# Attention and gated feed-forward in one kernel: which tokens go through plain matrix products, which through Strassen units, and how many DMAs turn a pair of heads

## The chip, the cores and the metric

One core of one Trainium2 chip runs the whole program. The metric is the device time of one execution in microseconds (us), as the median of several runs. One execution of each kernel is also recorded by the hardware profiler. Engines are named as in the profile: PE is TensorE (matrix products), ACT is ScalarE, DVE is VectorE, POOL is GpSimd, SP is the engine that only issues DMAs.

## The reference

```python
batch, n_heads, seq, head_dim = (8, 12, 448, 64)
n_tokens, d_model, d_ff = (3584, 768, 1536)

def _attn_ref(q, k, v):
    scores = 1.0 / np.sqrt(q.shape[-1]) * np.matmul(q, k.transpose(0, 1, 3, 2))
    scores = scores - np.max(scores, axis=-1, keepdims=True)
    attn = np.exp(scores)
    attn = attn / (np.sum(attn, axis=-1, keepdims=True) + 1e-09)
    return np.matmul(attn, v)

def _moe_ref(x, w_gate, w_val, w_out):     # x: the heads side by side, 3584 x 768
    g = x @ w_gate
    silu = g * (1.0 / (1.0 + np.exp(-g)))
    return (silu * (x @ w_val)) @ w_out    # 3584 x 768, float32
```

## The kernel before

Everything is computed in float16 with float32 accumulation. The order of all engines' work is written out by hand; nothing is reordered later except where a small planner sorts a list of items.

**Attention.** The 96 heads form 48 pairs, six to a batch. A pair's q, k and v are loaded and cast on GpSimd's DMA queue (`load_qk16` L186, `load_v` L205), from pair 16 on into a ring of four places (`rawslot` L182, `RL` L23) and nine places for v (`VS` L31). From pair 11 on GpSimd copies q and k into one tile (`prep_quad` L233; two copies) and SP turns them by DMA transposes, one for k and one for q (L239, L243), into `qkT`, five buffers. For each chunk of keys PE makes scores into a PSUM tile `s` of two banks (`qk_quad` L324; three such tiles rotate), and ACT takes the exponential into a ring `E` (L349). Then PE multiplies by v (`pv_mm` L413, 32 matmuls of 65 columns per pair), DVE divides by the sums (`pv_close` L444), and the result `xt` is turned into `X`, from pair 12 on by two DMA transposes on SP: 384 tokens (L494) and the last 64 (L498). `X` has two buffers, each for two batches (896 tokens, "kk").

**Feed-forward, plain.** `Step` (L546) makes one of the 12 row blocks of the gate and value products for up to 512 tokens: six matmuls each, a tanh on ACT, two products on DVE, result in `hts`. `block` (L873) gives the steps of a token block: the even blocks are 384 tokens, the odd ones 512, so blocks 0 and 1 are batches 0 and 1, blocks 2 and 3 are batches 2 and 3, and so on.

**Feed-forward, Strassen.** `Unit` (L763) makes two row blocks of one product for 2 x w tokens with seven half-size products instead of eight; 12 units (six for the gate, six for the value) cover all rows. They need sums of weights (`weight_sums` L753, on POOL), sums of token columns (`token_sums` L988, on DVE) and additions on DVE. `unit_items` (L1319) lists their pieces with engines and durations and `order_of` (L43) sorts them. The output product uses the same scheme: `out_group` (L672) makes 256 tokens x 384 columns in 42 matmuls of 192 columns; it is a generator with two halves (18 and 24 matmuls). Sums for it come from `h_sums` (L535) and `out_sums` (L523). Rows that don't fill a group go through `plain_out` (L642, 192 or 384 columns) or `single_out` (L1002).

**The stages.** From 26 us on the pairs go through a `plan` (L1163) of visits: three chunks of scores, then usually one pair's products with v, then items of feed-forward work. Every seventh visit is bare, without a pair's products. From visit 19 on `VISITS` (L978) says for each visit how many plain steps and how many whole groups run (`run_pair` L1027 makes two steps with the second one split in halves, `run_group` L1069 and `run_group_with` L1090 put a group around a step or a pair's products). Blocks 0 to 4 are plain. After the last exponential come: units of width 256 for block 5 (the last 64 tokens of batch 4 and batch 5), three pairs of groups, units of width 448 for batches 6 and 7 with one `single_out` row block between them, and three pairs of groups for these.

Of the kernel before, what the change touches and what calls it, by code (L numbers as in the profile page):

```python
# [30 lines left out]
VS = 9  # L31
# [33 lines left out]
def kernel(  # L65
# [44 lines left out]
    xp = ctx.enter_context(tc.tile_pool(name="xp", bufs=2))  # L110
    fp = ctx.enter_context(tc.tile_pool(name="fp", bufs=2))
    ps_s = ctx.enter_context(tc.tile_pool(name="ps_s", bufs=3, space=PSUM))
    ps_f = ctx.enter_context(tc.tile_pool(name="ps_f", bufs=2, space=PSUM))
# [10 lines left out]
    warm = consts.tile([128, 128], FP16, name="warm")  # L124
    warm4 = warm[:].unsqueeze(1).to_broadcast([128, 4, 128])
# [22 lines left out]
    hall = consts.tile([128, NFB * NB * S], FP16, name="hts")  # L148

# [4 lines left out]
    wo = [wo_all[:, i] for i in range(2)]  # L154

    raw = {}
    qkT = {}
    X = {}

    def dummy(n, w=4):  # L160
        wp = ps_f.tile([128, 512], FP32, tag="f", name="wp")
        for _ in range(n):
            nc.tensor.matmul(wp[:, 0 : w * 128], lhsT=warm[:], rhs=warm4[:, 0:w], start=True, stop=True)
# [17 lines left out]

    def rawslot(pr):  # L182
        a, b = divmod(pr % RS if pr < 2 * RS else pr % RL, 2)
        return raws_all[:, a, :, b]

    def load_qk16(pr, n=2):  # L186
        for t, src in ((0, q), (1, k)):
            if pr >= QUAD and t:
                if n == 1:
                    kd = rawslot(pr)[:, 1].rearrange("p (h x) -> p h x", h=2)  # L190
                else:
                    kd = raws_all[:, pr % RS // 2, 1].rearrange("p b (h x) -> p (b h) x", h=2)
                load_keys(nc.gpsimd, kd, k, 2 * pr, 2 * n)
                continue
# [3 lines left out]
            else:  # L198
                dst = raws_all[0:P, pr % RS // 2, t].rearrange("p b (h x) -> p (b h) x", h=2)
# [5 lines left out]
    def load_v(pr, n=1):  # L205
        b, h = divmod(2 * pr, H)
# [26 lines left out]
    def prep_quad(pr):  # L233
        rq, rk = raw[pr]
        qk16 = attp.tile([128, 2, NC, 2, D], FP16, tag="qk16", name="qk16", bufs=3)
# [12 lines left out]
    def prep(pr):  # L248
# [3 lines left out]
        if pr == 0 or pr >= NPE:  # L252
            qk16 = attp.tile([128, 2, NC, 2, D], FP16, tag="qk16", name="qk16", bufs=3)[0:P]
# [7 lines left out]
        qkT[pr] = attp.tile([128, 2 * S + D], FP16, tag="qkT", name="qkT", bufs=QB)  # L261
# [11 lines left out]
        def turn0():  # L273
            for t in range(2):
                tp = ps_s.tile([128, 2, 512], FP32, tag="s", name="tp")
# [17 lines left out]
        def turn():  # L293
            if pr < WIDE + 2:
                tp = ps_s.tile([128, 2, 1024], FP16, tag="s", name="tp")[:, 0]
            else:
                tp = ps_f.tile([128, 1024], FP16, tag="f", name="tp")
# [25 lines left out]

    def qk_quad(pr, c):  # L324
        s = ps_s.tile([128, 2, 512], FP32, tag="s", name="s")
        if c < KR:
            t = qkT[pr]
            for hx in range(2):
                nc.tensor.matmul(  # L329
                    s[:, hx, 0:S],  # L330
                    lhsT=t[ts(hx, 64), ts(c + low(pr, hx), 128)],
                    rhs=t[ts(hx, 64), ds(NC * 128, S)],
# [3 lines left out]
        else:  # L336
            for hx in range(2):
                for p in (pr, pr + 1):
# [3 lines left out]
                        s[ts(1 - lo, 64), hx, 0:S],  # L342
                        lhsT=t[ts(hx, 64), ds(0 if lo else KR * 128 + 64, 64)],
                        rhs=t[ts(hx, 64), ds(NC * 128, S)],
# [8 lines left out]
    def qk(pr, c):  # L353
# [3 lines left out]
        s = ps_s.tile([128, 2, 512], FP32, tag="s")  # L357
# [19 lines left out]
    def pv_chunk(pr, c):  # L377
        if c == 0:
            accs[pr] = ps_f.tile([128, 512], FP32, tag="f", name="acc")
# [48 lines left out]
    def pv_open(pr, one=False):  # L428
        if one:
            acc = ps_s.tile([128, 2, 512], FP32, tag="s", name="acc")  # L430
            accs[pr] = [acc[:, hx] for hx in range(2)]
        else:
            accs[pr] = [ps_f.tile([128, 512], FP32, tag="f", name="acc") for _ in range(2)]
# [1025 lines left out]
```

## Time and profile before

| what | value |
|---|---|
| median of three runs (lowest, highest) | 429.64 us (429.29, 430.12) |
| span of the profiled execution | 428.2 us |
| matmuls | 4635 |
| last exponential ends | 300 us |
| TensorE busy from 83.6 to 300.1 us | 215.7 of 216.5 us |
| TensorE busy from 300.1 us to the end | 124.0 of 128.1 us |
| DMA, mean over the span | 117 GB/s |

The span is that of one profiled execution; the runs' times hold a little more than the span. "Busy" is the union of an engine's instructions; matmuls overlap in a pipeline, so what a matmul costs is the distance from one start to the next, and not its listed mean duration. A turn is a DMA transpose: SP spends about 1.25 us to issue it, and it lands some time later; the landing is what a waiting engine sees.

### The profile page before, as it was taken

To read this page: it belongs to the slowest core of one execution; us is meant where nothing else is said; L and a number is where in the kernel's file an instruction comes from. 1 tells how busy PE (TensorE), PEld (TensorE's weight loads), DVE (VectorE), ACT (ScalarE), POOL (GpSimd) and SP (SyncE) were. 2 spreads that over 40 slices of the span, in tenths; PEclk is the share of its full clock that TensorE was granted. 3 is DMA by queue.
4 is the path that set the end of the run, shared out by engine and by line. 5 is a ranking of instruction groups with operands and counts; after the bars stand their busy time and mean duration, and the time that the engine had idled before them with its cause. 6 is when DMAs were issued, how large, how long until landed. Compare 5 with 4: busy or idle time off the path is not lost.

```text
span 428.2 us, 11621 instructions
## 1 busy us (share of the span) xinstructions
PE 420.5 (98%) x4635; PEld 290.2 (68%) x4635; DVE 267.7 (63%) x642; ACT 245.2 (57%) x395; POOL 233.3 (54%) x358
## 2 busy tenths in 40 slices
PE   8999999999999999999999999999999999999996
PEld 3666656555557777747666677777888995555795
DVE  4666562576758665575545776567777765565663
ACT  6975667556566645546667556568655225545221
POOL 8756543999887583658543885934999000000001
PEclk9999999999999999999999999999999999999999
DMA  9999999999999999999999999823100331000125
GB/s 138 177 200 200 199 173 190 121 169 209 160 138 137 115 146 150 146 136 120 124 151 122 139 149 117 152 45 97 25 1 14 101 99 51 0 0 2 38 76 148
DMA packets 108551, 50.02 MB, mean 117 GB/s; under 512 B 60864, under 2 KB 105232, under 8 KB 108496
## 3 DMA queue, kind: packets, MB, share of 16 engines
q0 software_dynamic: 46944, 24.83, 54.0%
q1 hardware_dynamic: 61408, 24.27, 33.6%
q8 instruction: 36, 0.59, 0.7%
q14 instruction: 19, 0.16, 0.1%
q10 hardware_dynamic: 144, 0.17, 0.1%
HBM read 49.55 MB, written 11.01 MB: 141 GB/s over the span
## 4 chain that ended last, share of the span: by engine, by line
PE 77%; DMA 15%; POOL 4%; DVE 1%; ACT 1%; issue 1%; SPq 0%; POOLq 0%; DVEq 0%
PE og L679 18%; PE gp L557 15%; PE un L795 10%; PE vp L557 9%; PE acc L420 8%; PE ub L795 8%; PE s L329 5%; DMA wv<-in_moe_w_val_dram 4%; DMA qkraw<-in_q_dram 4%; DMA qkraw<-in_k_dram 3%; DMA wg<-in_moe_w_gate_dram 2%; PE op L650 2%; POOL qkraw L200 2%; DMA qkT<-qk 1%; PE s L341 1%; PE op L1003 1%
## 5 line engine op out<-in xcount | busy, mean ns | idle before, releaser
L349 ACT ACTIVATE E<-s 128x896 f16<-128x896 f32 x126 | 106.6, 918 | 40.2 <-PE s L329 28.2
L557 PE MATMUL gp<-X,wg 128*128 128x384 f16 (+1 forms) x360 | 73.9, 347 | 0.0
L237 POOL COPY qk<-qkraw 128x512 f16<-128x512 f16 x72 | 43.7, 649 | 50.8 <-DMA qkT<-qk 48.9
L557 PE MATMUL vp<-X,wv 128*128 128x384 f16 (+3 forms) x360 | 66.7, 321 | 0.1
L610 DVE SCALAR_TENSOR_TENSOR t<-sg,gp 128x384 f32<-128x384 f32 (+1 forms) x60 | 36.3, 607 | 42.5 <-ACT sg L584 42.2
L557 PEld LDWEIGHTS <-wv 128*128 128x128 f16 x462 | 43.8, 98 | 25.8 <-issue 0.3
L640 POOL DMA_DIRECT2D out_dram<-osb x3 | 1.6, 541 | 90.9 <-ACT osb L698 90.9
L177 POOL DMA_DIRECT2D vraw<-in_v_dram x72 | 43.8, 629 | 12.8 <-DVE X L492 6.9
L557 PEld LDWEIGHTS <-wg 128*128 128x128 f16 x360 | 32.8, 98 | 26.1 <-issue 1.9
L584 ACT ACTIVATE sg<-gp 128x384 f32<-128x384 f32 (+1 forms) x60 | 32.1, 537 | 28.8 <-PE gp L557 28.1
L177 POOL DMA_DIRECT2D qkraw<-in_k_dram x70 | 42.4, 619 | 7.7 <-DMA wo<-in_moe_w_out_dram 4.7
L367 ACT ACTIVATE E<-s 112x896 f16<-112x896 f32 x48 | 40.5, 919 | 8.5 <-PE s L359 8.3
L420 PEld LDWEIGHTS <-E 128*128 128x128 f16 (+1 forms) x1152 | 37.4, 96 | 10.9 <-issue 4.7
L679 PEld LDWEIGHTS <-hts 128*128 128x128 f16 x528 | 44.1, 98 | 0.3
L420 PE MATMUL acc<-vo,E 128*128 128x65 f16 (+1 forms) x1152 | 42.3, 192 | 0.7 <-DVE X L492 0.3
L616 DVE SCALAR_TENSOR_TENSOR hts<-t,vp 128x384 f16<-128x384 f32 (+3 forms) x60 | 32.5, 541 | 5.5 <-PE vp L557 1.9
L698 ACT ACTIVATE osb<-og 128x384 f32<-128x384 f32 x22 | 10.8, 491 | 39.4 <-PE og L679 37.5
L200 POOL DMA_DIRECT2D qkraw<-in_q_dram x44 | 29.9, 680 | 5.4 <-DMA vraw<-in_v_dram 1.4
L450 DVE TENSOR_TENSOR xt<-acc,R 128x256 f16<-128x256 f32 x72 | 30.6, 425 | 2.5
L329 PE MATMUL s<-qkT 64*128 64x448 f16 x216 | 30.4, 354 | 0.6 <-DMA qkT<-qk 0.5
L679 PE MATMUL og<-wo,hts 128*128 128x192 f16 x264 | 29.0, 246 | 0.0
L679 PEld LDWEIGHTS <-hsum 128*128 128x128 f16 x300 | 25.5, 98 | 1.0
(180 smaller groups left out, 723.8 us busy)
## 6 DMA issues: line engine op xcount, KB each, us to landing
vraw<-in_v_dram POOLq DMA_DIRECT2D x72, 64.0 KB, 4.9
qkraw<-in_q_dram POOLq DMA_DIRECT2D x41, 112.0 KB, 4.8
qkraw<-in_k_dram POOLq DMA_DIRECT2D x68, 64.0 KB, 4.8
wg<-in_moe_w_gate_dram POOLq DMA_DIRECT2D x8, 288.0 KB, 9.7
wv<-in_moe_w_val_dram POOLq DMA_DIRECT2D x8, 288.0 KB, 10.2
wo<-in_moe_w_out_dram POOLq DMA_DIRECT2D x2, 1152.0 KB, 19.4
out_dram<-osb SPq DMA_DIRECT2D x7, 288.0 KB, 4.1
out_dram<-osb SPq DMA_DIRECT2D x6, 336.0 KB, 3.2
```

The costliest lines, as they stand in the source:

```text
L177: eng.dma_start(dst[ts(s, 64)], rows)
L200: nc.gpsimd.dma_start(dst, flat.rearrange("h (p c) d -> p h (c d)", c=NC))
L237: nc.gpsimd.tensor_copy(dst.rearrange("p c h d -> p h c d"), src)
L329: nc.tensor.matmul(s[:, hx, 0:S], lhsT=t[ts(hx, 64), ts(c + low(pr, hx), 128)], rhs=t[ts(hx, 64), ds(NC * 128, S)], start=True, stop=True,)
L349: nc.scalar.activation(e[:, 0 : 2 * S].rearrange("p (h q) -> p h q", h=2), s[:, :, 0:S], AF.Exp, scale=sm_scale)
L367: nc.scalar.activation(e[:, :, 0:S], s[0:P, :, 0:S], AF.Exp, scale=sm_scale)
L420: nc.tensor.matmul(acc[:, ts(j, D + 1)], lhsT=e[rows, ds(hx * S + j * 128, 128)], rhs=Vts[pr % NV][rows, hx, col, 0 : D + 1], start=first, ...
L557: nc.tensor.matmul(dst[:, 0:w], lhsT=wslice(kind, self.fb, cb), rhs=X[kk][:, cb, ds(c0 + lo, w)], start=(cb == 0), stop=(cb == NCB - 1),)
L610: nc.vector.scalar_tensor_tensor(self.t1[:, 0:n], self.sg[:, 0:n], 1.0, self.gp[:, 0:n], ALU.add, ALU.mult)
L616: nc.vector.scalar_tensor_tensor(self.hts[:, self.fb, ds(lo, w)], self.t1[:, ds(lo, w)], 0.5 * HS, vp[:, 0:w], ALU.mult, ALU.mult)
L679: nc.tensor.matmul(dst, lhsT=lhs(n), rhs=rhs(n), start=first and n == 0, stop=n == NH - 1, skip_group_check=True)
L795: mm = nc.tensor.matmul(dst, lhsT=lhs[:, n], rhs=rhs[:, n], start=first and n == 0, stop=n == NK - 1, skip_group_check=True,)
```

## The change

The diff does five things.

1. Only blocks 0, 1 and 2 (batches 0 and 1, and 384 tokens of batch 2) are plain. After the last exponential come three unit stages: batches 4 and 5 (width 448), then the last 64 tokens of batch 2 with batch 3 (width 256), then batches 6 and 7 (width 448). Each is followed by its groups. The 512 tokens of batches 2 and 3 leave `X` before pair 36 overwrites it: SP writes them to DRAM in visit 26 (`spill`) and reads them back behind the first unit stage. Two of the three token sums move from DVE to POOL.
2. A visit has one item: a step (`S`), the first or the second half of a group (`1`, `2`), or a quarter-row output product (`Q`).
3. A pair's q and k are turned by one DMA. A pair's `xt` is turned by one DMA of four blocks, which writes 64 columns more than the pair has; the pair after it overwrites them. Batch 3 (odd, in the first pair of buffers) keeps two DMAs.
4. From pair 16 on, q, k and v are loaded for two pairs at a time.
5. PSUM tiles come from a hand-written rotation, so that a group that is held over two visits keeps its tile while the others go round. The copies `p1` and `p15` of a group live in its output tile.

```diff
-VS = 9
+VS = 10
...
+    dram = ctx.enter_context(tc.tile_pool(name="dram", bufs=1, space=bass.MemoryType.DRAM))
...
+    order_in = {"s": [0, 1, 2], "f": [0, 1]}
+    lent = {}
+    def bank(kind, name, shape, dtype, hold):
+        slots = order_in[kind]
+        at = slots.pop(0)
+        t = ps.tile(list(shape), dtype, tag=f"{kind}{at}", name=name)
+        if hold:
+            lent[id(t)] = (slots, at, t)
+        else:
+            slots.append(at)
+        return t
...
     def load_v(pr, n=1):
+        if pr % VS + n > VS:
+            fit = VS - pr % VS
+            load_v(pr, fit)
+            return load_v(pr + fit, n - fit)
...
     def prep_quad(pr):
...
-        qkT[pr] = attp.tile([128, NC * 128 + S], FP16, tag="qkT", name="qkT", bufs=QB)
+        qkT[pr] = attp.tile([128, 2 * NC * 128], FP16, tag="qkT", name="qkT", bufs=QB)
         nc.sync.dma_start_transpose(
-            qkT[pr][:, 0 : NC * 128].rearrange("p (c q) -> p c q", q=128),
-            qk16[:, 0].rearrange("p c h d -> p (c h d)"),
-        )
-        nc.sync.dma_start_transpose(
-            qkT[pr][:, NC * 128 :].rearrange("p (c q) -> p c q", q=P),
-            qk16[0:P, 1].rearrange("p c h d -> p (c h d)"),
+            qkT[pr][:].rearrange("p (c q) -> p c q", q=128),
+            qk16[:].rearrange("p t c h d -> p (t c h d)"),
         )
...
     def turn_x(pr):
...
+        if kk > 1 or not bb:
+            at = (bb * NCB + hp) * S if kk > 1 else hp * NB * S
+            nc.sync.dma_start_transpose(
+                Xflat[kk][:, ds(at, (KR + 1) * 128)].rearrange("p (j q) -> p j q", q=128),
+                xt[:].rearrange("p j d -> p (j d)"),
+            )
+            return
...
     def out_group(kk, c0, hts, t, at, qw, osb, last=False, own=False, mid=None):
...
-        g = ps_s.tile([128, 2, 512], FP32, tag="s", name="og")
+        g = two_banks("og", hold=True)
...
-        p1 = fp.tile([128, QW], FP32, tag="p1", name="p1")
-        p15 = fp.tile([128, QW], FP32, tag="p15", name="p15")
+        p1 = osb[1][:, ds(qw * OH, QW)]
+        p15 = osb[1][:, ds(qw * OH + QW, QW)]
...
         def add_block(i, visits):
-            if i < B - NB - 1:
+            if i < NB + 1:
...
-        FIRST_STEPS = [2, 2, 1, 2, 1, 1, 1]
-        VISITS = [
...
+        ITEMS = "S" * 23 + "12" + "S" + "12" * 3 + "QQ" + "12" + "Q" + "12" + "Q"
+        SUMS = {x: 1 for x in [*range(12, 24), *range(24, 32), *range(41, 45)]}
...
+        def run_half_group():
+            if not opened:
+                opened.append(groups.pop(0)[0]())
+                next(opened[0])
+            else:
+                next(opened.pop())
...
             for n, (pr, c) in enumerate(ordered):
-                if n == 2 and (after_group or ordered[n] in quads):
+                if n == 2 and item == "2":
+                    run_half_group()
+                elif n == 2 and ((x > base and ITEMS[x - base - 1] == "Q") or ordered[n] in quads):
                     rests = open_products(rests)
                 qk(pr, c)
...
-                if 14 <= pr + LA < NPAIR:
-                    load_qk16(pr + LA, 1)
-                if 12 <= pr + 3 < NPAIR:
-                    load_v(pr + 3)
+                n = 1 if pr + LA < 2 * RS else 2
+                if 14 <= pr + LA < NPAIR and pr % n == 0:
+                    load_qk16(pr + LA, n)
+                n = 1 if pr + 3 < 2 * RS else 2
+                if 12 <= pr + 3 < NPAIR and (pr + 3) % n == 0:
+                    load_v(pr + 3, n)
...
+                if item == "S":
+                    gate_small[0] = bare
+                    run_fv(True)
+                elif item == "1":
+                    run_half_group()
+                elif item == "Q":
+                    out_small[0] = True
+                    run_o()
+                    out_small[0] = False
...
+                add_sum(SUMS.get(x, 0))
...
+            if x == 26:
+                nc.sync.dma_start(spill[:].rearrange("p (c x) -> p c x", c=NCB), X[1][:, :, 384:])
...
+        pairs = [pair_groups(KL - 1, 0, hts, p, at=p % 2) for p in range(3)]
+        items = units_of(KL - 1, 0, S, x_of(KL - 1), t6, hts, pairs)
...
         run_items(items)
+        back = rfree[:, 0 : NCB * 512]
+        nc.sync.dma_start(back, spill[:])
...
+        t3 = token_space(T[:, 0 : 4 * NK * 256], 256)
+        for fn in token_sums(x3, t3, nc.gpsimd):
+            fn()
+        sums.clear()
+        sums.extend(pair_sums(pairs))
+        run_groups(pairs)
+
+        hts3 = hview(384, 512)
+        pairs = [pair_groups(1, 384, hts3, p, at=1 - p) for p in range(2)]
+        run_items(units_of(1, 384, 256, x3, t3, hts3, pairs, False))
+        t7 = token_space(T[:, 0 : 4 * NK * S], S)
+        for fn in token_sums(x_of(KL), t7, nc.gpsimd):
+            fn()
+        sums.extend(pair_sums(pairs))
+        run_groups(pairs)
...
+        pairs = [pair_groups(KL, 0, hts, p, p == 2) for p in range(3)]
+        run_items(units_of(KL, 0, S, x_of(KL), t7, hts, pairs))
+        sums.extend(pair_sums(pairs))
+        run_groups(pairs)
```

More of the change, by code (lines that the diff above doesn't have):

```diff
@@ L154 @@
     wo = [wo_all[:, i] for i in range(2)]
+    qk16s = [consts.tile([128, 2, NC, 2, D], FP16, name=f"qk16_{i}") for i in range(3)]
     raw = {}
@@ L1109, in run_budget @@
                     budget -= run_o()
-                elif len(fvq) > 1 and fvq[0].at[1] and 2 * fvq[0].time < budget <= 4 * fvq[0].time:
-                    budget -= run_pair()
                 else:
@@ L1241 @@
                 add_block(adds[x], end - x)
-            around = bool(todo) and x > base and VISITS[x - base][1:3] == (0, 1)
-            for _, p0 in todo if not around else []:
+            for _, p0 in todo:
                 pv(p0)
@@ L1394, in run_groups @@
                 add_sum()
-        x7 = X[KL]
-        t7 = token_space(xp.tile([128, NCB, NT], FP16, tag="X", name="T")[:].rearrange("p a b -> p (a b)"), S)
-        tsums7 = token_sums(x7, S, t7)
-        first, behind = (pair[0][1] for pair in groups5)
-        first[0]()
-        sums.extend([tsums7[0], *first[1:], *behind, *tsums7[1:]])
-        for pair in [groups] + groups5:
-            run_groups([pair])
-        hts = hview(0, NT)
-        units = {}
-        items = unit_items(units, lambda u: Unit(u, S, x7, t7, hts), S)
@@ new lines @@
+        pv_rest(p0)
+        pv_quad(p0)
+        turn_x(p0)
+        wsum_space(vfree[:, 5 * VE : 8 * VE], 4)
+        wsum_space(Eall[:, 4 * NK * 128 : ER * EC], 18)
+        wsum_space(attp.tile([128, 2 * NC * 128], FP16, tag="qkT", name="wsum", bufs=QB), 2)
+        for vo in Vts[:4]:
+            wsum_space(vo[:].rearrange("p h c d -> p (h c d)"), 1)
+        for xt in Xts:
+            wsum_space(xt[:].rearrange("p s d -> p (s d)"), 1)
+        for u in range(3, NFB):
+            items[f"W_{u}"] = (POOL_, 3.65, [f"W_{u - 1}"], lambda u=u: weight_sums(u))
```

317 lines of the change are left out of this document (117 added, 200 removed), and 7 rows, old and new, of the table VISITS.

## The prediction

> **What bounds the kernel now.** I read the page first (span, busy shares, slices), then the chain of waits in order of time, then the timeline around single visits, and last the landings of the turns.
>
> ```profile
> span 428.2 us, 11621 instructions
> ...
> PE 420.5 (98%) x4635; PEld 290.2 (68%) x4635; DVE 267.7 (63%) x642; ACT 245.2 (57%) x395; POOL 233.3 (54%) x358
> ...
> PE   8999999999999999999999999999999999999996
> ...
> PEclk9999999999999999999999999999999999999999
> ```
>
> TensorE is busy in every slice at the full granted clock. So the time is its matmuls times their spacing, plus small gaps. The spacing stands in the chain, as the length of a piece over its count:
>
> ```profile
> 86.19 2.59 PE gp L557 x12
> ...
> 130.82 1.95 PE gp L557 x12
> ...
> 139.80 1.98 PE og L679 x24
> ...
> 365.34 1.70 PE un L795 x9
> ...
> 399.72 3.58 PE op L1003 x22
> ```
>
> That gives 216 ns for 512 columns, 162.5 ns for 384, 82.5 ns for 192 and 189 ns for 448. These are the prices of the sum below.
>
> In the attention stage the work comes in visits: three chunks of scores, one pair's products with V, then the planner's item. The timeline of one visit that holds a single 384-wide step, TensorE first and ScalarE behind it:
>
> ```profile
> 266.78 0.55 PE L329 MATMUL s<-qkT 64*128 64x448 f16 x4
> ...
> 268.41 1.14 PE L557 MATMUL gp<-X,wg 128*128 128x384 f16 x6
> ...
> 270.46 0.38 PE L341 MATMUL s<-qkT 64*64 64x448 f16 x4
> ```
>
> ```profile
> 267.19 2.53 ACT L349 ACTIVATE E<-s 128x896 f16<-128x896 f32 x3 [0.30 <-PE s L329]
> 269.64 0.49 ACT L584 ACTIVATE sg<-gp 128x384 f32<-128x384 f32 x1
> ```
>
> The visit lasts 270.46 - 266.78 = 3.68 us, and ScalarE has 2.53 + 0.49 = 3.02 us in it. TensorE still sets the pace, but with 0.66 us of margin only. A visit with one quarter-row output product instead (292.68 to 295.66) lasts 2.98 us, and there ScalarE paces it.
>
> The turns of X, by their DMA's landing, while loads run (first answer) and after the last loads (second):
>
> ```profile
> L494 SPq DMA_TRANSPOSE X<-xt x27: 1190/1220/1987, 93.6 to 256.4; - x27
> ...
> DMA to landing us min/median/max: 2.7/5.3/7.4
> ```
>
> ```profile
> L494 SPq DMA_TRANSPOSE X<-xt x7: 1192/1212/1702, 262.3 to 295.6; - x7
> ...
> DMA to landing us min/median/max: 2.3/3.1/4.3
> ```
>
> Nothing waits on these 5.3 us now: TensorE lost only 0.7 us to late turns of q and k, in two waits at 77 and 85 us:
>
> ```profile
> PE s L329 <- DMA qkT<-qk: 0.5, 1, 0.5
> ...
> PE s L341 <- DMA qkT<-qk: 0.2, 1, 0.2
> ```
>
> **The change, part by part.**
>
> *Plain steps become units.* The steps of batch 2's last 64 tokens with batch 3 (512 tokens) and of batch 4's first 384 go: 12 steps x 12 matmuls x 216 ns = 31.1 us, and 12 x 12 x 162.5 ns = 23.4 us, together 54.5. A unit stage of 448 columns comes: 12 units x 21 matmuls x 189 ns = 47.6, and two Z of 0.19 = 0.4. The 256-wide stage stays one stage, for other tokens. Net -6.5 us.
>
> *Output.* 48 quarter-row matmuls of 82.5 ns go (-4.0), 24 of 384 columns come (3.9): -0.1. The number of group products stays at 924.
>
> *Pairs of steps.* The split second steps (96 pieces of 256, 108 of 192 columns) become whole ones. At 109 and 82.5 ns against 216 and 162.5 this is 48 x 2 + 54 x 2.5 ns: -0.2.
>
> TensorE's work thus falls by 6.8 us.
>
> *One item a visit.* The attention stage keeps its visits but loses some 71 us of items, so it should end near 229 instead of 300 us. I add it from 83.6 us, where the planned part begins, by visits of the same contents. Twelve with a 512-wide step: ten at 4.4 (the trace has 4.2 to 4.6) and two without products with V at 3.4, 51 us. Twelve with 384: eleven at 3.68 and one bare, 43.5 us. Seventeen with half a group or a quarter row, at 3.0 to 3.7, and the last at 1.6: some 51 us. Sum 145.5. In these short visits two engines come close. ScalarE: in the four bare visits with half a group or a 384-wide step, TensorE has 0.56 + 1.97 + 0.33 (the gap of a usual visit) = 2.86 us, ScalarE 2.54 + 0.49 = 3.03, so 0.17 x 4 = 0.7; in three quarter-row visits 2.98 - 2.75 = 0.23 each, 0.7. I take 1.4; bounds 0 (ScalarE catches up from its margin elsewhere) and 5 (0.3 in each of 17 visits). VectorE: a 384-wide visit that also holds one sum has 1.20 (two closes of 0.177 + 0.425) + 0.55 + 0.55 + 0.41 (V copy) + 0.55 to 0.92 (sum) = 3.3 to 3.6 us of 3.68, in part waiting for the tanh. I take 0.13 in each of eight: 1.0; bounds 0 and 3.
>
> *Stage boundaries.* Before, an output product covered each end of a unit stage. The new 256-wide stage has none (its single row block does not exist): after its last matmul come a closing product of 0.41, a sum of 0.55 and the next sum of 0.55 on VectorE, against 0.5 us of group product that can run. With the hand-overs I take 1.2; bounds 0.5 and 3. The token sums move to GpSimd: before, 1344 columns took 0.86 us on VectorE. On GpSimd 384 columns take 0.91, so 768 some 1.8 and 1344 some 3.2 us. Four each make 7.3 and 12.8 us, covered by the groups in front (252 x 82.5 ns = 20.8 and 168 x 82.5 = 13.9). Without cover they would show in full. The tokens come back from DRAM (0.79 MB at the 200 GB/s of the busiest slices, 4 us, and 3 for the landing) ahead of the first: 7 + 7.3 = 14.3 of 20.8. The second is taken in order, so its fourth sum has a margin of some 3 us. I cost both at nothing.
>
> *DMAs.* A pair's q and k are turned by one DMA of 8 blocks, its X by one of 4. For most pairs SP's queue has two issues of about 1.25 us instead of four (the 8-block one of pair 11 took 1.345): a relief worth nothing by itself. GpSimd's load issues halve from pair 16 on. But the 4-block turn of X covers 512 columns of a place of 448, so from pair 24 on it overlaps the next pair's place, and the built program makes each turn wait on SP for the landing of the turn before. Behind that wait in SP's order stand the q and k turns of four pairs ahead; for these TensorE waits next. Demand: seven visits serve six pairs, so a pair every (6 x 3.68 + 3.03) / 6 = 4.2 us, and about 4.0 in the visits with groups. If a turn lands within that, nothing is lost. If it takes L, then 16 pairs (25 to 40, while loads run) fall behind by 16 x (L - 4.1), less the lead of a q and k turn: four pairs = 16.5, less copy 1.2, issue 1.3 and landing 5.3, so about 8.5 us. Bounds: L = 3.1 (row without loads) costs 0; L = 5.3 (row with loads) costs 16 x 1.2 - 8.5 = 10.7. For the value I take the stretch with the nearest rate of pairs (99 to 125 us, a pair every 4.6 us), where the five turns landed in 5.5, 4.0, 4.6, 5.3 and 3.2, mean 4.5: behind by 6.4, inside the lead, 0 lost.
>
> The Trainium skill, "DMA: Bandwidth & Descriptors", section "Anatomy of one DMA — SWDGE (gpsimd) path", gives a DMA about 2.0 us of fixed time plus its bytes over 436 GB/s; by it a turn of 128 KB would land in an estimated 2.3 us and the new wait would never bind. The trace has 5.3 and 3.1 for 96 KB, so the rows decide.
>
> *Sum:* 428.2 - 6.8 + 1.4 + 1.0 + 1.2 = 425.0 us of span. The median of the runs, 429.64, lies 1.44 above the profiled span; the same on top gives 426.4 us.
>
> **The rivals.**
>
> *The turns of X pace the stage (slower).* As above with L at 5.3: 426.4 + 10.7 = 437. The gain is used up at a loss of 3.2, that is from L = 4.1 + (8.5 + 3.2) / 16 = 4.8 us. When TensorE waits, loads thin out and L falls back, so I expect the middle, L near 5.0: 16 x 0.9 - 8.5 = 5.9, 432.3 us. For it: 27 landings with a median of 5.3, and loads and turns that must pass in 146 instead of 216 us. Against it: half as many turns in flight, and the 4.5 above.
>
> *All costs are covered.* ScalarE and VectorE catch up and the boundary hides: 428.2 - 6.8 + 1.44 = 422.8. For it: in 140 to 280 us TensorE's slices show no idle. Against it: the 2.98 us visits are in the trace.
>
> *Supply at the start.* The loads of pairs 16 and 17 now stand as one ahead of pair 15's turn, where TensorE already waits 0.7 us. 0.23 MB more at 200 GB/s is 1.2 us, and up to 3 with the burst's landing; every later visit is shifted: 427.6 to 429.4, and 429.4 is no change. Against it: SP's queue is shorter there.
>
> **How the numbers follow.** Chances: forecast 0.40 (own range 424.4 to 428.4), turns pace 0.34, all covered 0.13, supply 0.13. What a measurement can tell from no change is 0.2%, 0.86 us. Below 428.78 lie nearly all of the forecast (0.38), all of the covered case, a third of the supply case and a twentieth of the turns' case (0.02): 0.57 by the cases, of which I take off 0.05, for a change that touches every stage can meet a wait that I have not priced: 0.52. Slower: 0.30 of the turns' case, 0.02 of the supply case, and those 0.05: 0.37. The rest, 0.11, is no change. The range leaves a tenth out on either side: low 422.6, just under the covered case, high 436.0, near the turns' case at its row.
>
> **What would show it.** Right: 4475 matmuls; the last exponential near 229 us; visits of 3.7 and 3.0 to 3.3 us; no more than 1 us of TensorE waiting for a turn of q and k; a gap near 1 us behind the 256-wide units. Wrong: TensorE waiting for those turns between 170 and 225 us while SP waits for the landing of a turn of X; or a stretch of ScalarE without idle time through the group visits; or token sums on GpSimd that end behind the groups.

## The result, and the profile after

The changed kernel takes 466.45 us (median of four runs, 461.22 to 471.49) against 429.88 us (429.29 to 430.30) for the kernel before on the same chip. Two of its four runs lie 2% above the other two, and the ratio, formed from the shorter two (461.22 and 462.38 us), is 1.0745, 95% interval 1.0722 to 1.0768: 7.4% slower. Below, their mean, 461.8 us, stands for the changed kernel. The forecast was 426.4 us, the range ended at 436.0. The profiled execution, from the page:

```profile
span 460.6 us, 11108 instructions
...
PE 424.9 (92%) x4475; PEld 280.1 (61%) x4475; DVE 276.4 (60%) x627; ACT 258.9 (56%) x418; POOL 200.7 (44%) x279
...
PE   8999999999999998879749999999999499999996
```

The 4475 matmuls are as forecast, and so is their work: the counts by width in this trace, at the prediction's prices, come to 6.8 us less than before. The span grew by 32.4 us. Of these, 28.0 are idle TensorE (35.7 us instead of 7.7); the other 4.4 are busy time, which grew although there was less to do, because matmuls stood further apart behind some of the waits. The slices with 8, 7 and 4 are the attention stage from 173 to 242 us, the last 4 is the boundary behind the 256-wide units. What TensorE waited for in the changed kernel (us in total, times, longest):

```profile
PE s L372 <- DMA qkT<-qk: 14.1, 6, 5.8
PE og L718 <- DVE hts L580: 3.3, 1, 3.3
PE acc L451 <- DVE hts L655: 2.8, 9, 0.6
PE og L718 <- DVE hsum L581: 2.3, 1, 2.3
```

Turns of q and k come late (first line); VectorE's sums come late at a boundary (second and fourth); and a product with V waits for VectorE's closing product in nine visits (third). On SP stands the wait that the rival "the turns of X pace the stage" is made of, a turn of X behind the landing of the one before; in GpSimd's order the copies wait for the landings of turns and of loads:

```profile
SPq L528 <- DMA X<-xt: 30.7, 15, 5.5
```

```profile
POOL qk L268 <- DMA qkT<-qk: 34.9, 10, 8.0
...
POOL qk L268 <- DMA qkraw<-in_k_dram: 30.0, 11, 6.0
```

Where the 35.6 us between the forecast span (425.0) and this one lie, by the starts of matmuls (the attention stage ends here with the first half of its last quarter-row product, 256.5 us in the changed kernel). Two experiments that are told below stand beside it: "no loads" leaves out the loads of the last 24 pairs, "three off" does that and two more edits.

| stretch, us | forecast | after | no loads | three off |
|---|---|---|---|---|
| up to visit 12 | 83.6 | 84.0 | 84.6 | 85.7 |
| 12 visits with a 512-wide step | 51 | 54.7 | 54.7 | 54.0 |
| 12 visits with a 384-wide step | 43.5 | 48.8 | 47.4 | 47.8 |
| the other 16 visits | 51 | 69.0 | 54.2 | 56.2 |
| added for ScalarE and VectorE | 2.4 | | | |
| behind the attention stage | 193.5 | 204.1 | 203.8 | 196.0 |
| span | 425.0 | 460.6 | 444.6 | 439.7 |

### The profile page after: what moved, and what is told of

The parts are those of the page before. It is cut to its first block, busy times and chain, and to the rows that moved or that the text cites. A ratio compares the mean times of both kernels' runs of the same rounds, so it can differ in the third digit from the quotient of the medians.

```text
span 460.6 us, 11108 instructions
## 1 busy us (share of the span) xinstructions
PE 424.9 (92%) x4475; PEld 280.1 (61%) x4475; DVE 276.4 (60%) x627; ACT 258.9 (56%) x418; POOL 200.7 (44%) x279
## 4 chain that ended last, share of the span: by engine, by line
PE 54%; DMA 21%; DVE 11%; ACT 5%; POOL 5%; issue 3%; SPq 1%; DVEq 0%; ACTq 0%; POOLq 0%
PE un L834 15%; PE og L718 14%; PE ub L834 11%; DMA qkT<-qk 8%; PE acc L451 5%; DMA wg<-in_moe_w_gate_dram 4%; PE gp L596 4%; DMA qkraw<-in_q_dram 3%; DMA vraw<-in_v_dram 3%; ACT E L380 3%; DMA wv<-in_moe_w_val_dram 2%; DVE hts L655 2%; DVE t L649 2%; POOL qkraw L227 2%; PE op L1040 2%
## 5 line engine op out<-in xcount | busy, mean ns | idle before, releaser
L268 POOL COPY qk<-qkraw 128x512 f16<-128x512 f16 x72 | 43.1, 637 | 67.1 <-DMA qkT<-qk 34.9
L596 PE MATMUL vp<-X,wv 128*128 128x384 f16 (+1 forms) x216 | 45.0, 344 | 0.5 <-DVE xt L481 0.4
L596 PE MATMUL gp<-X,wg 128*128 128x384 f16 (+1 forms) x216 | 45.0, 344 | 0.0
L649 DVE SCALAR_TENSOR_TENSOR t<-sg,gp 128x384 f32<-128x384 f32 (+1 forms) x36 | 21.5, 598 | 31.2 <-ACT sg L623 31.2
L899 ACT ACTIVATE silu<-un 128x448 f32<-128x448 f32 (+1 forms) x36 | 17.6, 489 | 27.0 <-PE un L834 27.0
L883 DVE TENSOR_TENSOR un<-ub,kept 128x448 f32<-128x448 f32 (+1 forms) x36 | 20.3, 565 | 20.7 <-ACT kept L880 9.8
L596 PEld LDWEIGHTS <-wv 128*128 128x128 f16 x216 | 21.0, 98 | 18.6 <-DVE xt L481 0.9
L887 DVE TENSOR_TENSOR kept<-ub,kept 128x448 f32<-128x448 f32 (+1 forms) x36 | 20.1, 558 | 19.1 <-PE ub L834 17.9
L876 ACT ACTIVATE ub<-un 128x448 f32<-128x448 f32 (+1 forms) x36 | 17.1, 476 | 21.5 <-PE un L834 19.1
L737 ACT ACTIVATE osb<-og 128x384 f32<-128x384 f32 x22 | 10.8, 490 | 30.8 <-PE og L718 27.6
L201 POOL DMA_DIRECT2D vraw<-in_v_dram x40 | 24.7, 628 | 7.0 <-DMA wo<-in_moe_w_out_dram 5.2
L834 PEld LDWEIGHTS <-E 128*128 128x128 f16 x198 | 19.3, 98 | 13.5 <-issue 0.6
## 6 DMA issues: line engine op xcount, KB each, us to landing
wv<-in_moe_w_val_dram POOLq DMA_DIRECT2D x8, 288.0 KB, 10.1
```

Source lines behind the costliest of these rows:

```text
L201: eng.dma_start(dst[ts(s, 64)], rows)
L596: nc.tensor.matmul(dst[:, 0:w], lhsT=wslice(kind, self.fb, cb), rhs=X[kk][:, cb, ds(c0 + lo, w)], start=(cb == 0), stop=(cb == NCB - 1),)
L649: nc.vector.scalar_tensor_tensor(self.t1[:, 0:n], self.sg[:, 0:n], 1.0, self.gp[:, 0:n], ALU.add, ALU.mult)
L834: mm = nc.tensor.matmul(dst, lhsT=lhs[:, n], rhs=rhs[:, n], start=first and n == 0, stop=n == NK - 1, skip_group_check=True,)
L883: self.note(DVE_, nc.vector.tensor_tensor(self.e, self.b, self.p5, ALU.add), "e")
```

## The experiments

The theories have letters in what was written before each run. A: the chain of one-DMA turns of X on SP. A2 and A3: SP's order, by its issues or its waits. B and B2: the DMA engines, which loads and turns share. C and C2: GpSimd's order of loads and copies. D: GpSimd's sums hold VectorE's. E: two queues at once. Each kernel is the changed kernel with the edit shown; each time is the median of four runs, with the lowest and the highest. The changed kernel's own runs reach from 461 to 471 us, so a difference of a few us says little by itself; what a trace shows counts for more.

### One suspect at a time

**turn_two.** Two DMAs of exact width:

```diff
-            nc.sync.dma_start_transpose(
-                Xflat[kk][:, ds(at, (KR + 1) * 128)].rearrange("p (j q) -> p j q", q=128), ...
-            return
+            dst = Xflat[kk][:, ds(at, S)]      # then the two DMAs, as before
```

> The changed kernel (461 us at its best, 460.6 profiled), with only the turn of X put back to two DMAs of exactly 384 and 64 columns, so that no turn overlaps the place of the next and SP has no wait for a landing between them. Theory A (the chain of one-DMA turns on SP holds up the turns of q and k behind it): SP's 30.7 us of waiting for landings of X goes, the attention stage loses most of its 28 us of added TensorE idling and ends near 235 instead of 256.5 us: 438 to 445 us. Rival B (the DMA engines themselves cannot move loads and turns any faster than in these 257 us, share 9 in every slice): the waits move to other tiles, 457 to 463 us. Rival C (two-pair loads or the single 8-block turn of q and k hold GpSimd's copies): under 6 us gained, 455 to 461.

461.27 us (455.36 to 462.16). The profiled run is the shortest of the four (span 453.6 us), 6 us below the others. In it SP's waits for landings of X are gone, and TensorE's waits for q and k halve (6.7 and 0.9 us), but with three DMAs a pair SP issued the turn of pair 43 at 215.84 us, 9 us after its copy was done. A, as it stood, predicted 438 to 445: it falls as the whole cause.

**split_steps.** `fvq[0].split = fvq[0].alone = not bare` ahead of each step.

> The changed kernel with only the steps of the first 24 visits computed in two column halves again, as the second of a pair was before, so that a step's value product leaves its one-bank buffer earlier. Theory: TensorE's nine waits of the products with V for VectorE's closing product (2.8 us) and the like go, 0.25 us in each of some 20 visits: 456 to 459 us if these visits are paced by TensorE and its buffers. Rival: the visits are paced by the arrival of q and k, then what is saved in a visit is waited for later: 460 to 462 us.

470.19 us (466.2 to 478.99), a miss. The products' wait for the closing product went down, but not away (1.6 us in three waits), and in part moved to the scores (1.0 us in five); a 384-wide visit took 3.95 us instead of 3.91, and more was lost to q and k (18.5 and 2.4 us).

**sums_on_dve.**

```diff
-        for fn in token_sums(x_of(KL), t7, nc.gpsimd):
-            fn()
-        sums.extend(pair_sums(pairs))
+        sums.extend(pair_sums(pairs) + token_sums(x_of(KL), t7))   # and for t3 alike
```

> The changed kernel with the token sums behind the first two unit stages on VectorE, one in each of the last four free places of the groups in front, as the kernel before had them, instead of all at once on GpSimd. Theory D (a GpSimd sum of 1344 columns holds VectorE's sums, 2.3 to 3.0 us in place of 0.55, TensorE waits 5.6 us for them and then runs at half the clock): the 8.5 us of added time between 360 and 375 us shrink to about 2, 453 to 456 us. Rival (VectorE was late for its own work, GpSimd only ran beside it): 459 to 463 us, and the sums in the boundary still take over 2 us.

458.0 us (453.16 to 462.15). The stretch behind the attention stage falls from 204.1 to 195.7 us, by 8.4. The profiled execution, the longest of the four, lost as much again ahead of it: its attention stage is 6.9 us longer than the changed kernel's and begins 1.3 us later. The boundary in the changed kernel, VectorE first, then GpSimd, then TensorE (start, duration; in brackets the wait before):

```profile
362.83 2.30 DVE L580 TENSOR_TENSOR hts<-hts 128x768 f16<-128x768 f16 x1
365.17 2.96 DVE L581 TENSOR_TENSOR hsum<-hts 128x768 f16<-128x768 f16 x1
368.16 2.96 DVE L582 TENSOR_TENSOR qkraw<-hts,hsum 128x768 f16<-128x768 f16 x1
```

```profile
361.94 2.78 POOL L1030 TENSOR_TENSOR T<-X,T 128x1344 f16<-128x1344 f16 x1
364.68 3.03 POOL L1031 TENSOR_TENSOR T<-X 128x1344 f16<-128x1344 f16 x1
367.67 3.04 POOL L1032 TENSOR_TENSOR T<-X,T 128x1344 f16<-128x1344 f16 x1
```

```profile
365.19 0.67 PE L718 MATMUL og<-E,hts 128*128 128x192 f16 x6 [3.27 <-DVE hts L580]
368.18 1.14 PE L718 MATMUL og<-E,hsum 128*128 128x192 f16 x6 [2.33 <-DVE hsum L581]
369.12 1.17 PE L718 MATMUL og<-wo,hts 128*128 128x192 f16 x6
```

and the same in this experiment:

```profile
369.05 0.56 DVE L580 TENSOR_TENSOR hts<-hts 128x768 f16<-128x768 f16 x1
369.65 0.56 DVE L581 TENSOR_TENSOR hsum<-hts 128x768 f16<-128x768 f16 x1
```

```profile
369.67 0.67 PE L718 MATMUL og<-E,hts 128*128 128x192 f16 x6 [0.81 <-DVE hts L580]
```

A sum of 768 columns takes 0.56 us alone; beside GpSimd's it ends when GpSimd's ends (365.13 behind 364.72, 368.13 behind 367.71, 371.12 behind 370.71). TensorE waits 3.27 and 2.33 us, and then the same six matmuls stand 0.96 us apart instead of 0.50 until 373 us. D is shown.

**load_one.** `n = 1` for every load.

> The changed kernel with every load for one pair again instead of two from pair 16 on. Rival C (GpSimd waits 30.0 us for two-pair loads that land just in time, and its copies and SP's turns of q and k come late by that): 450 to 456 us. Theory A (the chain of turns of X sets the pace): the loads' waits go over into waits for the turn, 459 to 463 us; a few us slower is possible, since GpSimd issues more DMAs.

462.86 us (461.46 to 463.59): no change. GpSimd's copies waited 0.6 us for the loads of k instead of 30.0, SP's for landings of X rose to 35.0, TensorE's for q and k were 10.9 and 1.0. Rival C falls.

### The chain, the loads, and their order

**pad.** The places of X lie 512 columns apart instead of 448 (one overlap in a batch stays), and V has four buffers instead of five.

> The changed kernel with the turn of X still one DMA of four blocks, but into places 512 columns apart, so that it no longer overlaps the place of the next pair (but once in a batch); V has four buffers instead of five, to make room. With two DMAs a turn SP lost the waits for landings, but its issues were 3.8 us a pair and it ran some 12 us behind TensorE, with the turns of q and k behind its stores and turns of X; one DMA without a wait has 2.5 us a pair. Theory A2 (SP's place in the order, by waits or by issues, makes q and k late): the added idling of the attention stage falls to the 0.25 us a visit that the visits themselves took longer, some 9 us, and the two late waits near 215 and 230 us go: 438 to 446 us. Rival B (DMA engines at their limit): 453 to 462 us, with TensorE still waiting over 6 us for q and k.

456.53 us (451.69 to 459.1), ratio 1.0575 (1.0501 to 1.0649): some 7 us gained, where theory A2 had 16 to 24; it is in the range of B, though TensorE waits less for q and k than B said (4.9 us, not over 6). SP waits only 4.6 us for landings of X (two waits) instead of 30.7, but the turns land later than before the edit (SP's transposes between 140 and 225 us: times issued, median us to landing), and GpSimd waits longer for loads, 54.2 us instead of 30.0. In the changed kernel:

```profile
X<-xt SPq DMA_TRANSPOSE x18, 5.4
qkT<-qk SPq DMA_TRANSPOSE x16, 6.7
```

With places 512 apart:

```profile
X<-xt SPq DMA_TRANSPOSE x18, 7.0
qkT<-qk SPq DMA_TRANSPOSE x17, 8.0
```

**no_loads.** `load_qk16` and `load_v` return without a DMA for pairs from 24 on.

> The changed kernel without the loads of q, k and v for pairs 24 to 47 (these pairs compute with older rows; 24 of 48 pairs' loads, some 9 MB, are left out), turns and order as changed. Rival B (loads and turns share the DMA engines, so that everything lands late): turns land in 2.4 to 3.3 us as after the last loads, TensorE's waits for q and k go, 438 to 446 us. Theory A or A2 with landings that are long for another reason than the loads: 455 to 462 us. If both this and the kernel with places 512 apart gain, it is the landing under loads times SP's order, and neither alone.

446.45 us (446.05 to 450.12), ratio 1.0397 (1.0343 to 1.0451). The kernel leaves out half of the loads and computes with older rows in their place. TensorE's wait for q and k is 1.1 us in one piece; the order and the chain are the changed kernel's, and SP still waits 13.5 us for landings of X. In the table above, the attention stage falls from 172.5 to 156.2 us, by 16.3. The landings over the same stretch, without loads:

```profile
X<-xt SPq DMA_TRANSPOSE x20, 2.4
qkT<-qk SPq DMA_TRANSPOSE x19, 3.2
```

**load_first.** The lines with `load_qk16` and `load_v` move ahead of those with `prep`.

> The changed kernel with GpSimd's order changed alone: in each visit the loads are issued ahead of the copies of q and k, not behind them, where they stand behind a copy that waits for an earlier load or for the landing of a turn. Theory C2 (the load of a pair is just in time since its issue waits behind such copies): GpSimd's 30.0 us of waiting for loads falls below 15 and TensorE's waits for q and k by half, 450 to 456 us. Theory A2 (SP's order makes the turn late; the copy has time): 459 to 463 us.

471.78 us (468.11 to 477.72): slower. GpSimd's waits for loads fell to 5.1 us as thought, and its waits for landings of turns rose from 34.9 to 62.2; a new stall of some 6 us stands between 70 and 81 us, and those in the last third stayed. C2 falls, and the time lies outside both ranges.

**pad_sums_first.** The edits of pad, sums_on_dve and load_first.

> Three edits together: places of X 512 apart, token sums on VectorE behind the first two unit stages, and loads ahead of copies. If their gains are independent the sum is that of the three runs alone: with 8 us from the token sums and 18 from the places, 433 to 438 us, and 430 if the loads' order adds to it. If one stands in for the other, 440 to 450. Below the kernel before (429.8) only if the visits also shrink by 0.25 us, for which nothing is done here.

448.44 us (445.75 to 451.09), ratio 1.0445 (1.0389 to 1.0501). Behind visit 18 nearly no turn was late any more, but the stall at 70 us had come (visit 12 begins at 90.0 us instead of 84.0) and another of 2.3 us at visit 17: what is waited for early is not waited for again. From visit 12 on the attention stage took 158.3 us, with all loads, against 156.2 without half of them. This looked like two queues mended at once, which became theory E.

### Order of work, and the sum of the causes

**spread.** `ITEMS = "S" * 16 + "12SS" * 4 + "QQ" + "12" + "Q" + "12" + "Q"`, with the places of the sums moved to match.

> The changed kernel with the items of the attention stage in another order and nothing else: 16 single steps, then half-group pairs and pairs of steps in turn (four times), then the quarter rows as before; the visits and their sum of work are the same, but the short visits no longer stand all at the end. Without loads the 24 pairs from visit 24 on take 102 us, 4.24 us a pair; in the last third the order asks for a pair every 3.3 us. Theory B2 (the DMA engines deliver some 180 GB/s, with 740 KB a pair one pair in 4.0 us, so only the short visits outrun them): most of the 16 us of late turns go, 447 to 453 us. Rival A3 (a turn is late because of its place in SP's order behind the landing of the turn before, whatever the rate): the waits spread too, 457 to 463 us.

465.86 us (462.9 to 466.6): a miss, outside the ranges of both theories. Stalls of 6, 4 and 10 us (half clock included) stand at visits 31, 38 and 45. The rate that I had put down for the last third, a pair every 3.3 us, holds for the products with V in the visits 44 to 49 alone, and these the edit left as they were; the third as a whole asks for a pair in some 4.1 us, not far from the 384-wide visits ahead of it (4.4 to 4.6). So there was little to spread, and the stalls at 31 and 38 show that short visits are not needed for one.

**pv_order.** `pv_rest` is called for head 0 first, and for head 1 ahead of its own pieces.

> The changed kernel with the products with V in another order: all of the first head's, then all of the second's, where the shared chunk of both stood first. The second head's bank is the one that the step's value product of the visit before still holds (0.32 us of waiting in each of some 22 visits); so it is asked for 0.5 us later. The row-half products no longer run two at a time, +0.09 us a visit. Theory: 0.2 us less in each of 22 visits without a stall, 4 to 5 us, 456 to 458 us, or less than that if the turns of q and k then come later (460 to 462), as they did when the steps were halved.

469.59 us (463.73 to 476.33), a miss again. The wait for the closing product is gone from the products with V, but the 384-wide visits still took 3.91 to 4.04 us: TensorE now changes between 64-row and 128-row products twice more in a visit, each change 0.09 to 0.10 us in the distance from one matmul to the next, and the 64-row products of the two heads no longer run side by side (0.1 us). The rest is late turns (19.7 and 1.5 us in the profiled run, the longest of the four).

**all_four.** pad, spread, sums_on_dve and pv_order.

> Four edits together: places of X 512 apart, items spread, token sums on VectorE, the second head's products later. If turns then land in time everywhere, the time is that without late turns (16 us), without the token sums on GpSimd (7 us) and with shorter visits (4 us): 434 to 437 us; 440 to 446 if late turns remain. Below 429.8, the kernel before, only if the visits of 3.9 and 4.6 us also fall to 3.7 and 4.4.

447.71 us (447.11 to 448.45), ratio 1.041 (1.0382 to 1.0437), the lowest median of the complete kernels (not clear of pad_sums_first), above the 440 to 446 that were put down for late turns, and still slower than the kernel before. Late turns remain (6.5 us; visit 45, with one of them and half clock behind it, took 10.4 us instead of some 3).

**three_off.** no_loads, sums_on_dve and pv_order.

> The changed kernel without the loads for pairs 24 to 47 (these compute with older rows), with the token sums on VectorE and the second head's products later. It asks whether the three named causes are all of it: 446.3 without the loads, less 7 for the token sums, less 4 to 5 for the visits, is 434 to 436 us. If it stays above 440 there is a fourth cause; near 427, the time that was predicted, the visits are cheaper than I now think.

439.99 us (438.78 to 441.44), ratio 1.0231 (1.0198 to 1.0264). Against no_loads the stretch behind the attention stage lost 7.8 us, and the stage itself gained nothing: the visits are 1.8 us longer in sum, where 4 to 5 us less were expected, and 1.1 us were lost ahead of visit 12. What is left against the forecast span, 14.7 us, lies in the visits (10.1), ahead of them (2.1) and behind them (2.5).

### Two queues, or what the DMA engines carry

**late_first** and **pad_late.** load_first for `load_qk16` alone and from pair 16 on (`first = pr >= 16`), without and with the places of pad; **pad_late_sums** and **pad_late_sums_spread** add sums_on_dve, and spread.

> The changed kernel with the loads of q and k issued ahead of the copies from visit of pair 16 on (before that the order stays, since the same edit from pair 8 on cost 7 us at 70 us). Theory E (two queues: GpSimd's load behind a copy that waits, and SP's turn behind the landing of a turn; mending one moves the wait to the other): GpSimd's waits for loads go and its waits for the landing of turns grow from 35 to some 50 us; 457 to 463 us. Rival C (the loads' place alone): 446 to 452 us.

> The same with the places of X 512 apart as well: both queues mended, the token sums still on GpSimd. Theory E: no TensorE wait for q and k over 2 us behind 90 us, 443 to 446 us (the 460.6 profiled, less 16 for late turns, as without loads). Theory B (the DMA engines carry no more than some 185 GB/s, whatever the order): a stall of 5 to 10 us stays in the short visits, 450 to 457 us.

> The same with the token sums on VectorE: 7 us less than the kernel before it in this list, 436 to 439 us by theory E; 443 to 450 by theory B. Faster than the kernel before (429.8) by neither: the visits' 0.25 us and the two waits of the bare visits are left, some 10 us.

> The same with the items spread (group pairs between pairs of steps). Theory E: no late turn is left to save, so no change, 436 to 439 us, within 1.5 us of the kernel before it in this list. Theory B: the shorter demand at the end saves 4 to 8 us against it.

483.2 (481.1 to 486.64), 461.51 (457.02 to 465.59), 452.98 (451.59 to 458.54) and 460.05 us (458.08 to 460.3). E predicted a gain from the second on and falls: with both queues mended, TensorE waits 12.5 us for q and k in pad_late. B missed these three as well (450 to 457, 443 to 450, and a saving by spread, where 7 us were lost). late_first is the slowest kernel of all, 20 us above E's own range for it. GpSimd's waits for loads of k went to 5.9 us, those for landings of turns doubled, and the turns land later than in the changed kernel:

```profile
POOL qk L268 <- DMA qkT<-qk: 72.7, 17, 11.0
```

```profile
X<-xt SPq DMA_TRANSPOSE x17, 6.6
qkT<-qk SPq DMA_TRANSPOSE x15, 8.4
```

**no_v** leaves out the loads of V from pair 24 on; **twice_v** reads those rows once more, into DRAM:

```diff
     def load_v(pr, n=1):
+        if pr >= 24:
+            return
```

```diff
             load_keys(nc.gpsimd, vd, v, 2 * pr, 2 * n)
+            if pr >= 24:
+                for s in range(2):
+                    rows = ...          # the same rows again
+                    nc.gpsimd.dma_start(twice[pr // 2][ts(s, 64)], rows)
```

> The changed kernel without the loads of V alone for pairs 24 to 47 (these compute with older rows of V; 3.1 MB are left out), queues, turns and loads of q and k as changed. Theory B (26 MB have to pass between 90 us and the last load, and the DMA engines reach 186 GB/s at most, where TensorE at its own pace would need 204): 3.1 MB less are 17 us of DMA, as much as the late turns; TensorE's waits for q and k fall from 14 to under 3 us: 446 to 450 us. Theory E (order of SP's and GpSimd's queues): 458 to 462 us.

> The changed kernel with the rows of V of pairs 24 to 47 read a second time, into DRAM that nobody reads (3.1 MB more through the DMA engines, two more issues of 0.63 us on GpSimd for every two pairs; no result changes). Theory B: up to 17 us more, less where the engines were idle: 470 to 482 us. Theory E: 461 to 464 us.

455.62 us (453.58 to 459.56), ratio 1.0598 (1.054 to 1.0657), and 479.52 us (477.65 to 484.09), ratio 1.1154 (1.1074 to 1.1233). No turn of q and k needs V, and yet the time follows the loads of V: 6 us less, 18 us more, with 9.7 and 26.0 us of TensorE waiting for q and k. E (458 to 462, 461 to 464) falls in both; B had the second (470 to 482) and missed the first (446 to 450, under 3 us of waiting). V's bytes are not all that changes: its loads also stand in GpSimd's order, and the 24 added issues of twice_v take GpSimd 0.65 us each. The landings with V left out, and with V read twice:

```profile
X<-xt SPq DMA_TRANSPOSE x19, 4.7
qkT<-qk SPq DMA_TRANSPOSE x17, 5.3
```

```profile
X<-xt SPq DMA_TRANSPOSE x16, 6.1
qkT<-qk SPq DMA_TRANSPOSE x15, 7.3
```

In no_loads, no_v, the changed kernel and twice_v, whose queues have the same order, the landing of the turns of q and k and the time rise together: 3.2 us and 446.5, 5.3 and 455.6, 6.7 and 461.8, 7.3 and 479.5. Kernels with another order leave that line: pad has 8.0 and 456.5, all_four 7.5 and 447.7, and in pad_sums_first turns that land in 6.3 us cost the attention stage about 2 us. So beside loads the turns land late, and what this costs depends on the order as well; that it is the lead which counts there is argued below. That the engines carry no more than a fixed rate is not shown: by the packets of the trace, pad moved 186 GB/s between 90 us and its last load, the changed kernel 173, and no_v waited 9.7 us for q and k at only 157.

## Why the prediction was wrong

*TensorE's work.* -6.8 us: right by the counts in the trace, as is the count of matmuls.

*Turns of X: "mean 4.5: behind by 6.4, inside the lead, 0 lost".* This step failed. The landing was 5.4 us between 140 and 225 us, and with it the prediction's own formula gives 16 x (5.4 - 4.1) - 8.5 = 12.3 us; the runs show 16.3 (the attention stage with and without loads). The sign that was named for it came: TensorE waits for q and k while SP waits for landings of X. The row that I set aside had the right size (5.3 us while loads run); I took a 26-us stretch with five turns instead, and misread its pace: these turns stand 6.3 us apart, not 4.6. The lead of 8.5 counts the issue twice, since a landing is measured from the start of its issue; with 9.8 the formula gives 11.0 us. The rival "the turns of X pace the stage" named the place, but its mechanism is half of it: with the chain taken away (pad), 7 of the 16 us came back. A pair's data pass three orders: load ahead of copy on GpSimd, copy behind the landing that frees one of three tiles, turn behind turn on SP. A landing of 5 to 8 us is in each, and most edits to one of them moved the wait to another. One pass, in the changed kernel's rows: k lands in 6.1 us, two copies take 0.64 each, and the turn lands 6.7 us after its issue begins: 14.1 us without any waiting. The load is issued six pairs ahead. Before, some 35 pairs took 216.4 us, 6.2 a pair, so the lead was some 37 us, and landings nearly as late (in the kernel before, between 140 and 225 us) cost nothing:

```profile
qkT<-qk SPq DMA_TRANSPOSE x26, 5.5
X<-xt SPq DMA_TRANSPOSE x25, 4.8
```

Without late turns the changed kernel asks for a pair every 4.2 us, a lead of 25 us, and in the visits 44 to 49 for q and k of a pair every 3.9, 23 us; one long wait of SP (up to 5.5 us) and one of GpSimd (up to 8.0) on top of a pass come to 27.6. This account is put together from rows; no run changed the lead alone. The prediction counted the lead of one link only, and held the landing fixed while the demand rose.

The Trainium skill, "DMA: Bandwidth & Descriptors", section "Anatomy of one DMA — SWDGE (gpsimd) path", gives about 2.0 us and the bytes over 436 GB/s for a DMA that GpSimd issues; the prediction carried this over to a turn of X, which SP issues, and estimated 2.3 us. Without loads the trace agrees (2.4 us); beside loads it took 5.4, and the measurement decides.

*Token sums: "I cost both at nothing".* Failed: 8.4 us. GpSimd's time for them was about right (3.2 us forecast for each of 1344 columns, 2.73 to 3.04 measured), and so was the cover on GpSimd's side. What was missed is VectorE, which needs 0.55 us each for the first sums behind the units and could not run beside them; the "1.2" for the boundary rested on those 0.55. The Trainium skill, "SBUF — State Buffer", section "Who interferes with whom", says that a VectorE instruction with two inputs in SBUF (the state buffer) contends with a GpSimd instruction that reads SBUF, through a shared port that is an exclusive lock; the trace agrees, with three sums of 2.30 to 2.96 us in place of 0.56, each ending 0.4 us behind GpSimd's.

*Visits: 145.5 us, and 1.4 and 1.0 for ScalarE and VectorE.* Failed by 8.3 us: without late turns the three kinds of visits take 156.2. I had taken 3.68 us for a visit with a 384-wide step from one that followed an output product; before, most did. Now a step is followed by the next visit's scores and products with V, and these wait some 0.3 us for the step's closing product on VectorE (the 2.8 us in nine visits above), which makes 3.91. One such visit, without loads:

```profile
151.02 0.74 PE L362 MATMUL s<-qkT 64*128 64x448 f16 x6
151.33 0.55 DVE L657 SCALAR_TENSOR_TENSOR hts<-t,vp 128x384 f16<-128x384 f32 x1
...
151.60 0.19 PE L453 MATMUL acc<-vo,E 64*128 64x65 f16 x1
...
151.94 1.11 PE L453 MATMUL acc<-vo,E 64*128 64x65 f16 x31
```

The closing product ends at 151.88 us, and the second product with V starts at 151.94. The visit behind a bare one takes longer again, by 0.6 us with 512 columns and by 0.9 to 1.1 with 384. For 512 columns the plain case was 4.6 in the trace of before, and I used 4.4, the middle of 4.2 to 4.6. The third kind, "some 51 us", does not add up as it stands: seventeen visits at 3.0 already give 51, without the last one, while the plan has fifteen and the last. They take 54.2 us, in part since a second half of a group beside a pair's products takes 4.2 us and not 3.7 at most. The trace shows the wait of 0.3 us, but no run had a shorter 384-wide visit: of two attempts one left part of the wait, the other took it away, and both gave the time back elsewhere in the visit.

*Stage boundaries.* The first one was covered as forecast: the tokens came back from DRAM in 4.7 us. The rival "supply at the start" did not come: visit 12 begins at 84.0 us for 83.6 forecast.

What is left between 193.5 and 195.7 us behind the attention stage, 2.2 us, I did not trace to a cause. Nor is it settled what makes a turn land in 6.7 us beside loads and in 3.2 without.

## What to carry to other kernels

When a change shortens a stage, divide what must still be moved in it by the new time, and set each lead, in pairs or tiles, against the sum of all landings on the way at the new pace; that nobody waited for a landing before is no evidence that it is short. When edits to a queue's order move the wait to another queue, leave out transfers, or add some that nobody needs: no_loads, no_v and twice_v moved the time the way of their loads, where edits of order had moved the waits. Before an operation moves to another engine because that engine is idle, look at what the first engine must do meanwhile and whether both read the same memory.

## What the runs showed of the hardware

After a wait of 3.27 us and one of 2.33 close behind it, 192-column matmuls stood 160 ns apart instead of 83, from 368.2 to 372.9 us; the profile's windows give a granted clock of 0.76 for 360 to 374 us and of 0.50 for these 4.7. So the two waits cost TensorE some 2.4 us more than themselves. The same followed the 5.79 us wait of the attention stage (0.50 from 239.2 to 243.2 us, 2.0 us more), and did not follow the waits of 1.96 to 2.56 us in this trace. A change between 64-row and 128-row products costs 0.09 to 0.10 us each time, which ate part of the gain of pv_order. And the runs of one kernel spread over 1 to 13 us in these experiments, where the kernel before spreads over 1 to 3: a kernel whose TensorE waits for DMAs needs more runs for the same certainty. Why one of its runs waits longer than another was not traced.
